# A planned attention and gMLP kernel: the last gelu product of z2 with its sums on VectorE, the centred squares on ScalarE, a longer age for side work

## The chip, the cores and the metric

One core of a Trainium2 chip runs one program. Its engines run side by side, each with an instruction queue of its own that is worked off in order: TensorE (PE: matmuls, and PEld, the load of their weights), VectorE (DVE), ScalarE (ACT), GpSimd (POOL) and SyncE (SP), which here only starts transfers. The metric is the time of one execution on the device in microseconds, the median of several. TensorE alone writes the accumulators in PSUM; POOL reads and writes SBUF only.

## The reference

A block with two branches on the same normalised input is computed, in fp32: attention with 32 heads of 16 columns, and a gMLP whose gate mixes along the sequence. Shapes: x is 2048 x 512, half of the MLP's width is 896.

```python
xn = _layernorm(x)
q, k, v = split(xn @ wqkv)                       # 32 heads, Dh = 16
p = _softmax(q @ k.T * Dh ** -0.5)
attn = merge(p @ v) @ wo
z = _gelu(xn @ w_in)                             # tanh form
z1 = z[..., :Fh]
z2 = _layernorm(z[..., Fh:])
g = w_sp @ z2 + b_sp
return x + attn + (z1 * g) @ w_out
```

The layer norm of z2 is where the change is: mean and variance run over the 896 columns of gelu(z).

## The kernel before

**Precision and slots.** A dense product is made of three fp32r matmuls of high and low parts. Two such matmuls run at a time on the two halves of TensorE's rows: that is a *dense pair* (line 1216), into the accumulator `dps`. A block of scores (`scores`, line 1157) or of row maxima (`maxima`, line 1171) is a pair as well, into one of three PSUM tiles `sl`. ScalarE takes the exponentials of the scores (`pf`), VectorE the maxima (`mm`, line 872); each then frees its `sl`.

**The cycle.** The program is written by a planner in Python. It keeps a clock for each engine and lays out one order for all of them; on the chip only semaphores decide the times. The strings of ORDER say how a *cycle* goes: 8 blocks of scores (S), 7 blocks of maxima in a *short* cycle and 9 in a *long* one (M), 24 dense pairs among them (D), then the P·V block (V, `values`, line 1258): four rounds of matmuls over 8 tiles of exponentials. There are 128 cycles, one behind the other, counted here from 0 by the ends of their P·V blocks. Where no dense pair is ready the planner writes either nothing or a *filler* (line 1230), a pair of matmuls with the zero tile `zeror`. The time of a P·V block, in which neither new scores nor maxima are made, is called a *gap* below, since ScalarE and VectorE have room in it.

**Stages.** The dense work runs through a queue of generators: v and q, k (to cycle 12), z2 (`z2_all`, one tile of 128 rows a cycle, 16 tiles from cycle 13), z1 (`z1_all`), the spatial product in four column blocks of `w_sp` (`spatial`, with tiles `wsp` and `zs` loaded ahead), the output projection of the MLP (`mlp_out`) and of attention (`attn_out`). At the end the last four blocks of heads and the outputs follow (`last_pair`, `last_mm`, `last_add`).

**Side work.** What follows a dense product is a generator as well: `yield "A", t` asks for t microseconds of ScalarE, `"D"` of VectorE, `"G"` of POOL, `"C"` waits for a condition such as a free buffer. `advance` starts, at each planned moment, the task that is ready, by priority. Side work (priority 2) on ScalarE and VectorE (GATED) is gated by `may`: it starts only in a gap, or once it has waited longer than AGE:

```python
return k[3] < 2 or k[0] not in GATED or window[0] <= s0 <= window[1] or s0 - k[2] > AGE
```

**z2.** For a tile `z2_out` copies the two halves out of `dps` (ScalarE and VectorE), and `z2_norm` does the rest: x², its polynomial, the tanh, the product, statistics, r = 1/sqrt, the normalised tile in two column parts as high and low parts (`z2hl`), and their stores to `z2scr`, which SP issues. Each tile holds two of the 19 buffers `big` (`z`, and `u` until the gelu is done); `z2_all` starts a further tile only while more than one is free.

Of the kernel before, what the change touches and what calls it, by code (L numbers as in the profile page):

```python
# [8 lines left out]
F32 = mybir.dt.float32  # L9
F32R = mybir.dt.float32r  # L10
AF = mybir.ActivationFunctionType
ALU = mybir.AluOpType
# [4 lines left out]
P = 128  # L17
S = 2048
D = 512
H = 32  # L20
DH = 16
FH = 896
# [7 lines left out]
EPS = 1e-5  # L30
# [30 lines left out]
def fused_block(ctx, tc, x, wqkv, wo, w_in, w_spT, b_sp, w_out, out):  # L61
    nc = tc.nc
# [3 lines left out]
    sm = ctx.enter_context(tc.tile_pool(name="small", bufs=1))  # L66
# [10 lines left out]
    def act(out, in_, func, **kw):  # L77
        return nc.scalar.activation(out, in_, func, **kw)  # L78

    def ta(n):  # L80
        return 0.2 + n / 1220.0
# [69 lines left out]
    def after(us, fn, *args):  # L151
        at(ends[0] + us, fn, *args)
# [15 lines left out]
    def open_(tag):  # L168
        return "C", lambda: room[tag] > 0

    def lease(tag, n):
        room[tag] += n
# [58 lines left out]
    def hilo(nm):  # L231
        return big.tile([P, 2, 512], F32R, tag="hilo", name=nm, bufs=3)
# [267 lines left out]
    def z2_out(t, z, j):  # L500
        if j == 0:
            yield "A", ta(448)
            act(z[:, 0:448], dps[:, 0, :448], AF.Copy)
        else:
            yield "D", td(448)
            nc.vector.tensor_copy(z[:, 448:896], dps[:, 1, :448])
        rel()
        if not held[0]:
            spawn(z2_norm(t, z), 2, ends[0] + 0.08)

    def z2_norm(t, z):
# [12 lines left out]
        nc.gpsimd.tensor_scalar(u, u, 1.0, 1.0, ALU.add, ALU.mult)  # L524
        yield "G", 2.1
        nc.gpsimd.tensor_mul(z, u, z)
        lease("big", 1)
        st = sm.tile([P, 2, 6], F32, tag="zst", name=f"zst{t}", bufs=6)
        mv = sm.tile([P, 2], F32, tag="zmv", name=f"zmv{t}", bufs=6)
        rs = sm.tile([P, 3], F32, tag="zrs", name=f"zrs{t}", bufs=6)  # L530
        for j in range(2):
            yield "D", 0.62
            nc.vector.bn_stats(st[:, j, :], z[:, j * 448:(j + 1) * 448])
        yield "D", 0.1
        nc.vector.bn_aggr(mv, st)
        yield "G", 1.6
        g = nc.gpsimd
        v, r, q, m = rs[:, 0:1], rs[:, 1:2], rs[:, 2:3], mv[:, 0:1]
        g.tensor_scalar(v, mv[:, 1:2], 1.0, 4 * EPS, ALU.mult, ALU.add)
        g.tensor_tensor(r, v, mhalf, ALU.pow)  # L540
        g.tensor_scalar(q, r, r, v, ALU.mult, ALU.mult)
        g.tensor_scalar(q, q, -0.5, 1.5, ALU.mult, ALU.add)
        g.tensor_mul(r, r, q)
        g.tensor_scalar(q, m, r, -1.0, ALU.mult, ALU.mult)
        for j, (lo, w) in enumerate(((0, 512), (512, 384))):
            yield open_("hilo")
            lease("hilo", -1)
            hl = hilo(f"z2hl{t}_{j}")
            yield "G", 0.0012 * w
            g.tensor_scalar(hl[:, 0, :w], z[:, lo:lo + w], r, q, ALU.mult, ALU.add)  # L550
            yield "G", 0.0012 * w
# [490 lines left out]
    with tc.manual_schedule(engines=engines):  # L1042
# [259 lines left out]
        while n_pv < N or queue or tasks or late or urgent or turn or slots:  # L1302
            t = T["P"]
# [74 lines left out]
```

## Time and profile before

| what | value |
|---|---|
| median of 3 runs | 1856.94 us (1855.68 to 1857.37) |
| the profiled execution | 1855.84 us |
| its span, first to last instruction | 1853.9 us |
| mean granted clock of TensorE | 0.999 |
| ScalarE, exponentials `pf`, 1024 of them | 1026 ns each |
| ScalarE, Square and tanh of a z2 tile | 946 and 953 ns |
| transfers, mean rate | 165 GB/s |

The profile's page gives busy time and count for each engine, the chain of work that ended last, and groups of instructions of one line with their shapes: `out<-in`, count, busy time in all, mean of one in ns, and the idle time of the engine before them with what ended it. A view of stretches gives, for windows that are asked for, length, busy time and count in the order PE, PEld, DVE, ACT, POOL, then TensorE's granted clock, the share of the DMA engines and GB/s. A timeline row has start, duration, engine, line, operation, and in brackets the idle time before it. The clock is full in every stretch that is used here, so it plays no part.

### The profile page before, as it was taken

How to read it: one execution, taken by the hardware profiler on the slowest of the kernel's cores; microseconds unless marked ns; L12 is line 12 of the kernel's file. 1: busy time of each engine (PE TensorE's matmuls, PEld its weight loads, DVE VectorE, ACT ScalarE, POOL GpSimd, SP SyncE). 2: the span in 40 equal slices, each digit the busy share in tenths (PEclk: the TensorE clock that was granted, in tenths of full speed). 3: DMA queues.
4: the chain of work that ended last, by engine and by line, in shares of the span. 5: the costliest groups of instructions: out<-in, count | busy, mean ns of one | idle time of the engine just before them, and what ended most of it. 6: DMA issues, size and time to landing. Idle time of an engine off the chain costs nothing.

```text
span 1853.9 us, 38030 instructions
## 1 busy us (share of the span) xinstructions
PE 1807.5 (97%) x14778; PEld 1093.5 (59%) x14778; DVE 1440.9 (78%) x1677; ACT 1189.6 (64%) x1292; POOL 722.0 (39%) x808
## 2 busy tenths in 40 slices
PE   6999999999999999999999999999999999999998
PEld 4766566655655565556556665666656556565543
DVE  6578778888888787877878787787778878787883
ACT  2157777687776777666666665666656666565665
POOL 5324342778888777222452135102522240002200
PEclk9999999999999999999999999999999999999999
DMA  7728872533565246656867558565767667575422
GB/s 236 288 93 283 277 238 87 127 91 112 133 217 137 100 119 201 152 160 154 219 171 199 156 180 217 155 146 154 194 164 186 177 173 148 149 175 143 130 86 80
DMA packets 212124, 306.14 MB, mean 165 GB/s; under 512 B 36816, under 2 KB 108048, under 8 KB 209056
## 3 DMA queue, kind: packets, MB, share of 16 engines
q1 hardware_dynamic: 202824, 273.83, 53.8%
q0 software_dynamic: 9120, 29.89, 4.7%
q8 instruction: 116, 1.90, 0.4%
q14 instruction: 64, 0.52, 0.1%
HBM read 193.80 MB, written 109.85 MB: 164 GB/s over the span
## 4 chain that ended last, share of the span: by engine, by line
PE 87%; DVE 5%; DMA 2%; ACT 2%; issue 1%; POOL 1%; SPq 1%; DVEq 0%; ACTq 0%; POOLq 0%
PE dps L1216 35%; PE sl L1258 23%; PE sl L1157 14%; PE sl L1171 12%; DVE mm L872 3%; SPq L134 1%; PE dps L1230 1%; ACT pf L78 1%; DMA zs<-z2scr 1%; POOL wsp L293 0%; DMA wsp_11r<-in_w_spT 0%; PE sl L247 0%; PE sl L246 0%; PE sl L245 0%; PE sl L1016 0%
## 5 line engine op out<-in xcount | busy, mean ns | idle before, releaser
L872 DVE TENSOR_REDUCE mm<-sl 128x2 f32<-128x1024 f32 x1024 | 1223.8, 1222 | 202.2 <-PE sl L1171 195.8
L78 ACT ACTIVATE pf<-sl 128x1024 f32<-128x1024 f32 x1024 | 1041.6, 1026 | 335.1 <-PE sl L1157 298.5
L1258 PE MATMUL sl<-pf,vall 128*32 128x512 f32 x4096 | 467.9, 595 | 1.0 <-DVE on L1006 0.6
L1157 PE MATMUL sl<-qst,kst 50*128 50x512 f32 x2048 | 436.0, 418 | 9.4 <-DVE mm L872 2.9
L1171 PE MATMUL sl<-kst,qst 48*128 48x512 f32 x2048 | 422.1, 405 | 4.5 <-DVE mm L872 2.4
L1216 PE MATMUL dps<-wsp,zs 64*128 64x512 f32 x2352 | 379.0, 392 | 1.6 <-DMA zs<-z2scr 1.5
L1157 PEld LDWEIGHTS sl<-qst,kst 50*128 50x128 f32 x2048 | 194.3, 184 | 221.9 <-issue 79.6
L1258 PEld LDWEIGHTS sl<-pf,vall 128*32 128x32 f32 x4096 | 119.3, 109 | 266.9 <-issue 234.3
L1171 PEld LDWEIGHTS sl<-kst,qst 48*128 48x128 f32 x2048 | 195.1, 185 | 105.0 <-ACT pf L78 52.6
L1216 PEld LDWEIGHTS dps<-wsp,zs 64*128 64x128 f32 x2352 | 226.9, 187 | 39.3 <-DMA zs<-z2scr 2.2
L78 ACT ACTIVATE e<-sl 128x512 f32<-128x512 f32 x64 | 38.3, 598 | 205.2 <-PE sl L1258 198.0
L1280 DVE TENSOR_TENSOR e<-sl,e 128x512 f32<-128x512 f32 x64 | 44.3, 692 | 134.3 <-PE sl L1258 76.3
L778 POOL TENSOR_TENSOR hhl<-z1i,hhl 128x512 fp32r<-128x512 f32 x28 | 36.1, 1297 | 267.1 <-ACT hhl L78 267.0
L1216 PE MATMUL dps<-w,xt 64*128 64x448 f32 x768 | 110.4, 368 | 1.5
L1216 PE MATMUL dps<-wout,hp 64*128 64x512 f32 x672 | 110.5, 393 | 0.0
L923 POOL TENSOR_TENSOR ob<-ob 128x512 f32<-128x512 f32 (+1 forms) x16 | 20.6, 1285 | 195.2 <-DMA ob<-rscr 195.2
L1216 PEld LDWEIGHTS dps<-w,xt 64*128 64x128 f32 x768 | 73.5, 186 | 16.3 <-issue 7.8
L1216 PEld LDWEIGHTS dps<-wout,hp 64*128 64x128 f32 x672 | 65.8, 187 | 9.2
L919 POOL TENSOR_TENSOR ob<-ob 128x512 f32<-128x512 f32 (+1 forms) x16 | 20.6, 1287 | 101.6 <-DMA ob<-escr 100.9
L443 POOL TENSOR_TENSOR qkhl<-qr,qkhl 128x512 fp32r<-128x512 f32 x24 | 30.3, 1282 | 70.4 <-ACT qkhl L78 66.3
L1216 PE MATMUL dps<-wf,zs 64*128 64x512 f32 x336 | 55.5, 393 | 0.1
L1216 PE MATMUL dps<-xnT,wqk 64*128 64x512 f32 x288 | 47.7, 396 | 1.1 <-ACT vall L78 0.4
(289 smaller groups left out, 1688.3 us busy)
## 6 DMA issues: line engine op xcount, KB each, us to landing
zs<-z2scr SPq DMA_DIRECT2D x192, 256.0 KB
escr<-e SPq DMA_DIRECT2D x60, 256.0 KB
hscr<-hhl POOLq DMA_DIRECT2D x28, 512.0 KB, 6.4
qst<-qscr SPq DMA_DIRECT2D x30, 384.0 KB
kst<-kscr SPq DMA_DIRECT2D x30, 384.0 KB
qscr<-qkhl SPq DMA_DIRECT2D x16, 512.0 KB
kscr<-qkhl SPq DMA_DIRECT2D x16, 512.0 KB
xscr<-xnT POOLq DMA_DIRECT2D x16, 512.0 KB, 4.8
```

What stands on the lines that cost most here:

```text
L78: return nc.scalar.activation(out, in_, func, **kw)
L134: nc.sync.dma_start(raw(dst), raw(src))
L443: nc.gpsimd.tensor_sub(hl[:, 1, :], raw_, hl[:, 0, :].bitcast(F32))
L778: nc.gpsimd.tensor_sub(hl[:, 1, :], z1, hl[:, 0, :].bitcast(F32))
L872: nc.vector.tensor_reduce(mmax[g][:, :, t, kc], sl[k], AX.X, ALU.max)
L919: nc.gpsimd.tensor_add(both_[rows, 0, :], both_[rows, 0, :], both_[rows, 1, :])
L923: nc.gpsimd.tensor_mul(both_[rows, 0, :], both_[rows, 0, :], both_[rows, 1, :])
L1157: nc.tensor.matmul(sl[k][:, j, :], kst[p % 2][rows, kt * P:(kt + 1) * P], qst[p % 2][rows, c * 512:(c + 1) * 512], start=True, stop=True)
L1171: nc.tensor.matmul(sl[k][:, j, :], qst[p % 2][rows, tt * P:(tt + 1) * P], kst[p % 2][rows, kc * 512:(kc + 1) * 512], start=True, stop=True)
L1216: nc.tensor.matmul(dps[:, bank, :w], lhs, rhs, start=go, stop=stop)
L1258: nc.tensor.matmul(sl[k][cols:cols + VW, 0, :], vpack(kt + r, 2 * p + j), pf[:, j * 512:(j + 1) * 512], start=n % CYC == 0, stop=n % CYC = ...
L1280: nc.vector.tensor_add(e, sl[k][:, 0, :], e)
```

## The change

Three things in the text of the program:

1. In `z2_norm` the last product of the gelu, (tanh + 1)·z, moves from POOL (a pass over 896 columns and a product) to VectorE: one `scalar_tensor_tensor` for each half of 448 columns, which also gives the half's sum. BN_STATS and BN_AGGR go. POOL makes minus the mean of the two sums, ScalarE squares the tile less its mean and sums that, and POOL's short chain for r uses this sum. The buffer `u` is kept until the squares are done.
2. The microseconds that the planner takes for POOL's steps of z2 are changed.
3. AGE goes from 6 to 9, for all side work on ScalarE and VectorE.

```diff
-AGE = 6.0
+AGE = 9.0
...
-        yield "G", 1.0
+        yield "G", 0.98
         nc.gpsimd.tensor_scalar(u, u, 0.044715, 1.0, ALU.mult, ALU.add)
-        yield "G", 2.1
+        yield "G", 2.2
         nc.gpsimd.tensor_mul(u, u, z)
         yield "A", ta(FH)
         act(u, u, AF.Tanh, scale=GC)
-        yield "G", 1.2
-        nc.gpsimd.tensor_scalar(u, u, 1.0, 1.0, ALU.add, ALU.mult)
-        yield "G", 2.1
-        nc.gpsimd.tensor_mul(z, u, z)
+        st = sm.tile([P, 5], F32, tag="zst", name=f"zst{t}", bufs=6)
+        rs = sm.tile([P, 3], F32, tag="zrs", name=f"zrs{t}", bufs=6)
+        g = nc.gpsimd
+        a, b, m, square, v = (st[:, i:i + 1] for i in range(5))
+        for j, half in enumerate((a, b)):
+            cols = slice(j * 448, (j + 1) * 448)
+            yield "D", 0.63
+            nc.vector.scalar_tensor_tensor(z[:, cols], u[:, cols], 1.0, z[:, cols], ALU.add, ALU.mult, accum_out=half)
+        yield "G", 0.6
+        g.tensor_scalar(m, a, b, -1.0 / FH, ALU.add, ALU.mult)
+        yield "A", ta(FH) + 0.2
+        act(u, z, AF.Square, bias=m, accum_out=square)
         lease("big", 1)
...
-        for j in range(2):
-            yield "D", 0.62
-            nc.vector.bn_stats(st[:, j, :], z[:, j * 448:(j + 1) * 448])
-        yield "D", 0.1
-        nc.vector.bn_aggr(mv, st)
-        yield "G", 1.6
...
+        yield "G", 2.2
+        r, q = rs[:, 1:2], rs[:, 2:3]
+        g.tensor_scalar(v, square, 1.0 / FH, 4 * EPS, ALU.mult, ALU.add)
...
-        g.tensor_scalar(q, m, r, -1.0, ALU.mult, ALU.mult)
+        g.tensor_mul(q, m, r)
...
-            yield "G", 0.0012 * w
+            yield "G", 0.0009 * w + 0.32
...
-            yield "G", 0.0025 * w
+            yield "G", 0.0022 * w + 0.24
```

The planner writes another order with it. Three places:

TensorE, the beginning of cycle 22 in the z2 stage, behind the last row of a P·V block (`pf`, `vall`). `qst`/`kst` to `sl` are scores and maxima, `w` and `xt` the weights and the input of a z2 tile. Before:

```order
L1258 MATMUL sl_203<-pf_4471,vall 32x512 x2
L1157 MATMUL sl_202<-qst_90,kst_92 128x512 x2
L1171 MATMUL sl_201<-kst_93,qst_91 128x512 x2
L1230 MATMUL dps<-brow,zeror 128x512 x2
L1157 MATMUL sl_203<-qst_90,kst_92 128x512 x2
L1230 MATMUL dps<-brow,zeror 128x512 x2
L1171 MATMUL sl_202<-kst_93,qst_91 128x512 x2
L1230 MATMUL dps<-brow,zeror 128x512 x2
```

and now:

```order
L1257 MATMUL sl_201<-pf_4492,vall 32x512 x2
L1156 MATMUL sl_203<-qst_90,kst_92 128x512 x2
L1170 MATMUL sl_202<-kst_93,qst_91 128x512 x2
L1215 MATMUL dps<-w_0_0_2669,xt_4184 128x448
L1215 MATMUL dps<-w_0_1_2670,xt_4184 128x448
L1215 MATMUL dps<-w_0_0_2669,xt_4184 128x448
L1215 MATMUL dps<-w_0_1_2670,xt_4184 128x448
L1156 MATMUL sl_201<-qst_90,kst_92 128x512 x2
```

Where cycle 22 had 14 fillers and no dense pair, it has the 24 pairs of a tile and one filler. Counted to the end, the stage has no empty cycle any more and the later stages stand one cycle earlier. At the starts of column blocks 1, 2 and 3 of the spatial product, where before a cycle of 19, 19 and 16 dense pairs stood ahead of two or three cycles with 26 or 27, two cycles of 12 stand ahead of ordinary ones at blocks 1 and 2, and none at block 3; from cycle 89 on the dense work stands one cycle later than before. In all there are 146 matmuls on `zeror` in place of 206.

ScalarE and VectorE, the gap behind a short cycle of the z2 stage. `z2u` are the squares and tanh of a tile, `zst` the sums, `e` the partial output of the P·V block. ScalarE before, from the last exponential of the cycle on:

```order
L78 ACTIVATE pf_4303<-sl_202 128x1024
L78 ACTIVATE z_7_4202<-dps 128x448
L78 ACTIVATE z2u_4320<-z_7_4202 128x896
L78 ACTIVATE z2u_4136<-z2u_4136 128x896
L78 ACTIVATE e_2_4346<-sl_201 128x512
L78 ACTIVATE pf_4362<-sl_203 128x1024
```

and now:

```order
L78 ACTIVATE z_7_4189<-dps 128x448
L78 ACTIVATE pf_4311<-sl_202 128x1024
L78 ACTIVATE z2u_3982,zst_4167<-z_5_3856,zst_4167 128x896
L78 ACTIVATE z2u_4153<-z2u_4153 128x896
L78 ACTIVATE z2u_4315<-z_7_4189 128x896
L78 ACTIVATE e_2_4360<-sl_202 128x512
L78 ACTIVATE pf_4379<-sl_201 128x1024
```

Three side activations stand in the gap where two stood. On VectorE two tiles share such a gap; the second half of one and both halves of the next, now:

```order
L871 TENSOR_REDUCE mm_4635<-sl_202 128x2
L530 SCALAR_TENSOR_TENSOR z_8_4370,zst_4668<-z2u_4486,z_8_4370 128x448
L530 SCALAR_TENSOR_TENSOR z_9_4522,zst_4833<-z2u_4648,z_9_4522 128x448 x2
L1279 TENSOR_TENSOR e_3_4693<-sl_203,e_3_4693 128x512
L871 TENSOR_REDUCE mm_4635<-sl_201 128x2
```

Before, up to four BN_STATS and two BN_AGGR stood there. The first half of the one tile stands in the gap behind the long cycle.

TensorE, the end of the program (`sel`, `on` and `e` belong to the last heads). Before:

```order
L1258 MATMUL sl_201<-pf_20006,vall 32x512 x2
L1258 MATMUL sl_201<-pf_20014,vall 32x512 x2
L1230 MATMUL dps<-brow,zeror 128x512 x2
L1016 MATMUL sl_202<-sel,on_19792 128x512 x2
L1016 MATMUL sl_203<-sel,on_19916 128x512 x2
L1000 MATMUL sl_201<-e_3_19966,sel 32x128 x8
L1230 MATMUL dps<-brow,zeror 128x512 x8
```

and now:

```order
L1257 MATMUL sl_202<-pf_19905,vall 32x512 x2
L1257 MATMUL sl_202<-pf_19913,vall 32x512 x2
L1215 MATMUL dps<-wo_18339,op_1_19695 128x512 x2
L1015 MATMUL sl_203<-sel,on_19674 128x512 x2
L1015 MATMUL sl_201<-sel,on_19811 128x512 x2
L999 MATMUL sl_202<-e_3_19861,sel 32x128 x8
L1215 MATMUL dps<-wo_18339,op_1_19695 128x512 x4
L1215 MATMUL dps<-wo_18340,op_1_19695 128x512 x6
```

The last dense pairs of `attn_out` now stand behind the last P·V block, where fillers stood.

More of the change, by code (lines that the diff above doesn't have):

```diff
@@ L522, in z2_norm @@
         act(u, u, AF.Tanh, scale=GC)
-        yield "G", 1.2
-        nc.gpsimd.tensor_scalar(u, u, 1.0, 1.0, ALU.add, ALU.mult)
-        yield "G", 2.1
-        nc.gpsimd.tensor_mul(z, u, z)
-        lease("big", 1)
-        st = sm.tile([P, 2, 6], F32, tag="zst", name=f"zst{t}", bufs=6)
-        mv = sm.tile([P, 2], F32, tag="zmv", name=f"zmv{t}", bufs=6)
-        rs = sm.tile([P, 3], F32, tag="zrs", name=f"zrs{t}", bufs=6)
-        for j in range(2):
-            yield "D", 0.62
-            nc.vector.bn_stats(st[:, j, :], z[:, j * 448:(j + 1) * 448])
-        yield "D", 0.1
-        nc.vector.bn_aggr(mv, st)
-        yield "G", 1.6
-        g = nc.gpsimd
-        v, r, q, m = rs[:, 0:1], rs[:, 1:2], rs[:, 2:3], mv[:, 0:1]
-        g.tensor_scalar(v, mv[:, 1:2], 1.0, 4 * EPS, ALU.mult, ALU.add)
+        st = sm.tile([P, 5], F32, tag="zst", name=f"zst{t}", bufs=6)
[10 more added lines that the diff above has]
+        act(u, z, AF.Square, bias=m, accum_out=square)
+        lease("big", 1)
+        yield "G", 2.2
+        r, q = rs[:, 1:2], rs[:, 2:3]
+        g.tensor_scalar(v, square, 1.0 / FH, 4 * EPS, ALU.mult, ALU.add)
         g.tensor_tensor(r, v, mhalf, ALU.pow)
@@ L548, in z2_norm @@
             hl = hilo(f"z2hl{t}_{j}")
-            yield "G", 0.0012 * w
+            yield "G", 0.0009 * w + 0.32
             g.tensor_scalar(hl[:, 0, :w], z[:, lo:lo + w], r, q, ALU.mult, ALU.add)
-            yield "G", 0.0012 * w
+            yield "G", 0.0009 * w + 0.32
             g.tensor_scalar(z[:, lo:lo + w], z[:, lo:lo + w], r, q, ALU.mult, ALU.add)
-            yield "G", 0.0025 * w
+            yield "G", 0.0022 * w + 0.24
             nc.gpsimd.tensor_sub(hl[:, 1, :w], z[:, lo:lo + w], hl[:, 0, :w].bitcast(F32))
```

## The prediction

> **What bounds the kernel now.** First the page's busy line, the chain of work that ended last, and VectorE's largest group of instructions (busy us in all, mean ns, idle before it and what ended it).
>
> ```profile
> span 1853.9 us, 38030 instructions
> ...
> PE 1807.5 (97%) x14778; PEld 1093.5 (59%) x14778; DVE 1440.9 (78%) x1677; ACT 1189.6 (64%) x1292; POOL 722.0 (39%) x808
> ...
> PE 87%; DVE 5%; DMA 2%; ACT 2%; issue 1%; POOL 1%; SPq 1%; DVEq 0%; ACTq 0%; POOLq 0%
> ...
> L872 DVE TENSOR_REDUCE mm<-sl 128x2 f32<-128x1024 f32 x1024 | 1223.8, 1222 | 202.2 <-PE sl L1171 195.8
> ```
>
> TensorE is on the chain for 87% of the span. Its 97% needs care, since a matmul that sits in the pipeline counts as busy. So I cut the trace at the ends of the P·V blocks into 128 cycles and read the view of stretches, one cycle to a row (us; busy time and count for each engine). A short cycle has 7 blocks of maxima, a long one 9; both have 8 blocks of scores and 3.57 us of P·V. What varies is the number of dense pairs and of filler pairs. The rows, in order: cycles 22 to 25 (z2 stage), 39 and 40 (z1 stage), 45 to 47, and two ordinary ones of the spatial stage.
>
> ```profile
> 409.82:423.21 13.39, 13.15 (x98) 6.01 (x95) 12.51 (x17) 8.09 (x8) 12.39 (x21) 1.00 0.39 116
> 423.21:436.19 12.98, 12.77 (x115) 8.31 (x111) 9.57 (x10) 10.91 (x12) 12.25 (x18) 1.00 0.35 99
> 436.19:450.65 14.46, 14.10 (x121) 8.71 (x117) 12.91 (x17) 8.42 (x9) 13.22 (x17) 1.00 0.42 124
> 450.65:464.65 14.00, 13.65 (x119) 8.56 (x116) 10.65 (x13) 12.04 (x14) 7.40 (x9) 1.00 0.32 91
> 646.14:659.43 13.29, 13.21 (x115) 8.00 (x111) 9.13 (x8) 10.22 (x12) 9.59 (x11) 1.00 0.47 160
> 659.43:673.25 13.82, 13.73 (x118) 8.08 (x114) 12.61 (x16) 9.71 (x11) 9.46 (x11) 1.00 0.78 173
> 727.64:740.83 13.19, 13.19 (x117) 8.23 (x113) 8.49 (x7) 9.73 (x11) 12.86 (x15) 1.00 0.71 208
> 740.83:754.27 13.44, 13.42 (x102) 6.57 (x98) 11.87 (x15) 8.16 (x8) 6.98 (x8) 1.00 0.66 204
> 754.27:766.78 12.51, 12.51 (x104) 6.48 (x100) 8.31 (x7) 8.53 (x9) 5.16 (x6) 1.00 0.22 58
> 996.35:1009.29 12.94, 12.94 (x114) 8.08 (x110) 8.93 (x9) 8.70 (x9) 1.28 (x1) 1.00 0.68 146
> 1009.29:1022.95 13.66, 13.66 (x120) 8.16 (x116) 11.94 (x15) 8.18 (x8) 3.90 (x4) 1.00 0.68 185
> ```
>
> Two regimes are seen. In the last two rows the cycle is made of TensorE's slots: 8 + 9 + 24 + 1 filler = 42 pairs in 13.66 - 3.57 = 10.09 us, 0.24 us a pair; 39 pairs in 12.94 - 3.57 = 9.37 us give 0.24 again. But a cycle with few dense pairs doesn't get much shorter: with none at all and 14 fillers it is 13.39 (first row), with 12 and 4 fillers 13.44. There the maxima (L872, 1.222 us each, 9 of them 11.0 us) and the three slots `sl` set the pace. An empty cycle is therefore worth about 1 us itself, and costs the 24 pairs (5.8 us) that have to be done in another one.
>
> The first row is the stall that the change is near: no dense pair is issued in cycle 22, and POOL is busy for 12.39 of its 13.39 us.
>
> **The change part by part.** *POOL.* Per z2 tile it loses the pass of L524 and the product of L526, and gets one operation on 128x1.
>
> ```profile
> L524 POOL TENSOR_SCALAR z2u<-z2u 128x896 f32<-128x896 f32 x16 | 15.0, 940 | 31.7 <-ACT z2u L78 31.5
> L526 POOL TENSOR_TENSOR z<-z2u,z 128x896 f32<-128x896 f32 x16 | 33.8, 2110 | 0.3
> ```
>
> That is 0.94 + 2.11 = 3.05 us less in each of 16 tiles, less what the small one takes: some 45 us of the 218 that POOL works in the z2 stretch (below). None of it is on the chain by itself; it ends the empty cycle 22, as the order shows.
>
> *VectorE.* Out: two BN_STATS and a BN_AGGR; in: two SCALAR_TENSOR_TENSOR on 448 columns with both inputs in SBUF.
>
> ```profile
> L533 DVE BATCH_NORM_STATS2 zst<-z 128x6 f32<-128x448 f32 x32 | 18.9, 611 | 3.1 <-POOL z L526 3.1
> ...
> L756 DVE SCALAR_TENSOR_TENSOR z1i<-dps,z1i 128x512 f32<-128x512 f32 x24 | 15.4, 685 | 3.5 <-PE dps L1216 3.5
> ...
> L915 DVE TENSOR_TENSOR os<-os x16: 176/181/1032, 818.0 to 1761.8; 128x32 f32<-128x32 f32 x12, 96x32 f32<-96x32 f32 x4
> ...
> 898.86 1.27 POOL L778 TENSOR_TENSOR hhl<-z1i,hhl 128x512 fp32r<-128x512 f32 x1 [22.03 <-ACT hhl L78]
> 899.15 1.03 DVE L915 TENSOR_TENSOR os<-os 128x32 f32<-128x32 f32 x1
> ```
>
> L756 is the nearest form; at 448 columns 685 x 448/512 = 0.60 us, plus something for the sum: 0.62. The other bound is in L915, the one DVE operation of the long stages with both inputs in SBUF: 0.18 us in the median, but 1.03 where it began under a POOL operation, and it ended with that one (898.86 + 1.27 = 900.13; 899.15 + 1.03 = 900.18). So a hold by POOL can add 0.85, and the upper bound is 1.47 us. I take 0.62 for the operation and holds as below. The Trainium skill ("SBUF — State Buffer", section "SBUF: two separate sides") says that VectorE with two SBUF inputs and GpSimd take one port pair in turn, whole instructions at a time; these rows agree (1.03 against 0.18). By that rule any of the 32 could be held, at most 32 x 0.85 = 27 us of VectorE's time.
>
> What of it reaches TensorE depends on the room in the P·V block, where nearly all of these operations stand. Two such gaps of before, after a short and after a long cycle:
>
> ```profile
> 464.84 0.69 DVE L1280 TENSOR_TENSOR e<-sl,e 128x512 f32<-128x512 f32 x1 [1.21 <-PE sl L1258]
> ...
> 477.94 0.62 DVE L533 BATCH_NORM_STATS2 zst<-z 128x6 f32<-128x448 f32 x1
> 479.89 1.23 DVE L872 TENSOR_REDUCE mm<-sl 128x2 f32<-128x1024 f32 x1 [1.33 <-PE sl L1171]
> ...
> 462.11 0.94 ACT L78 ACTIVATE z2u<-z2u 128x896 f32<-128x896 f32 x1
> ...
> 465.22 1.02 ACT L78 ACTIVATE pf<-sl 128x1024 f32<-128x1024 f32 x1 [1.33 <-PE sl L1157]
> ...
> 461.08:464.65 3.57, 3.57 (x35) 0.94 (x34) 2.51 (x6) 2.70 (x3) 1.31 (x5) 1.00 0.02 5
> 475.54:479.11 3.57, 3.57 (x34) 0.93 (x32) 2.99 (x5) 0.00 (x0) 3.49 (x4) 1.00 0.17 42
> ```
>
> VectorE is free for 1.21 us in the first gap and 1.33 in the second. In the first, three of the new operations (1.86) stand where three BN_STATS (1.83) and two small BN_AGGR stood, and POOL works only 1.31 of 3.57; in the second, where POOL works 3.49 of 3.57, one stands for one BN_STATS, and a hold of 0.85 fits into 1.33. Queued behind them are the sum of the partial outputs (L1280) and the next maxima, for which TensorE waits.
>
> *ScalarE.* One Square with a sum more per tile. Lower bound 0.94 (the same function without a sum). Upper bound, should the sum be read out by an instruction of its own, plus the smallest ACTIVATE of the kernel:
>
> ```profile
> L344 ACT ACTIVATE rs<-mv,epst 128x2 f32<-128x2 f32 x8 | 2.4, 295 | 22.1 <-DVE mv L342 22.1
> ```
>
> so 0.94 to 1.24, against 1.33 us free in the first gap. It fits, barely; behind it stand the exponentials. For both engines I take **+1.0** in all (0 if everything fits; up to 1.4 in each of 8 gaps, 11, if each VectorE operation takes its upper bound: 3 x 1.47 - 1.83 - 1.21 = 1.4).
>
> *The gate (AGE).* In the order 102 of ScalarE's 112 side activations (those that read no PSUM) stood in a P·V gap already, so that the gate has ten to move, in 128 cycles. I cost it at nothing: the gaps hide them, and without that cover an activation among the exponentials is 0.6 to 0.9 us that the next one is late, mostly in ScalarE's own idle time. The stores of z2 (`z2scr`, issued by SP) and all other transfers are the same in number and kind.
>
> *The order that comes of it.* Matmuls are the same in number, but for the fillers: 206 rows of `zeror` before, 146 now, 30 pairs less.
>
> ```profile
> 285.09:577.82 292.73, 285.19 (x2344) 172.50 (x2340) 239.62 (x294) 211.61 (x234) 217.89 (x271) 1.00 0.47 133
> 507.33:577.82 70.49, 67.66 (x544) 38.51 (x540) 56.56 (x69) 49.08 (x55) 62.01 (x84) 1.00 0.67 201
> 914.77:982.65 67.88, 67.75 (x572) 40.80 (x569) 51.97 (x57) 44.16 (x46) 34.48 (x37) 1.00 0.65 178
> 1130.05:1200.06 70.01, 68.36 (x570) 41.02 (x566) 50.94 (x55) 43.43 (x45) 17.24 (x18) 1.00 0.67 166
> 1306.68:1390.35 83.67, 83.15 (x691) 49.62 (x687) 63.02 (x72) 52.01 (x54) 28.47 (x29) 1.00 0.69 176
> 1143.04:1159.74 16.70, 15.11 (x125) 8.91 (x122) 12.44 (x17) 8.14 (x8) 1.26 (x1) 1.00 0.66 148
> 1361.82:1377.41 15.59, 15.20 (x124) 8.99 (x121) 12.93 (x17) 9.09 (x10) 6.76 (x7) 1.00 0.63 161
> 954.79:969.26 14.47, 14.36 (x126) 8.69 (x122) 12.39 (x17) 8.16 (x8) 1.29 (x1) 1.00 0.57 134
> ...
> 1151.66 0.50 PE L1216 MATMUL dps<-wsp,zs 64*128 64x512 f32 x1 [1.17 <-DMA zs<-z2scr]
> ```
>
> I price the new cycles by the rows of their class.
> - Cycles 13 to 33 (z2 and the start of z1) took 292.73. Now: 7 short cycles without filler at 12.98, one with two at 14.00, 8 long ones at 14.46, then three short at 13.3 and two long at 13.85: 90.9 + 14.0 + 115.7 + 67.6 = 288.2, a gain of 4.5. The last five took 70.5 before (the second row), with waits for fetched rows; half of that difference may come back: **-3.0**.
> - Starts of a column block: cycles 59 to 63 took 67.88; now 13.19 + 13.44 + 12.51 + 13.66 + 12.94 = 65.7. 75 to 79 took 70.01; now 12.51 + 13.44 + 12.94 + 13.5 + 13.19 = 65.6. 88 to 93 took 83.67; now 13.5 + 13.19 + 13.66 + 12.94 + 13.5 + 13.19 = 80.0. (13.5: 41 pairs, 13.66 less one.) Together -10.3. Two of their cycles were longer than their class: 76 (16.70) and 92 (15.59) against 14.47 of cycle 62, all long and with 27 dense pairs. The excess, 2.2 + 1.1 = 3.4, is waits for transfers (the last row shows one) that the new order may meet as well; I give half of it back: **-8.6**.
> - The output projection of the MLP (cycles 102 to 117) has a filler in every long cycle before and none now: 7 x 0.24: **-1.7**.
> - The end: dense work is one cycle late from cycle 89 on, so that 18 pairs now stand in the last two cycles where 19 fillers were, 24 pairs against 19, 1.2 us; and one more sum (L967, the row below) stands among the last ones on VectorE. Partly side by side: **+2.0** (1.2 to 2.4).
>
> ```profile
> L967 DVE TENSOR_TENSOR fin<-dps,fin 128x1024 f32<-128x1024 f32 x8 | 9.7, 1216 | 0.7 <-PE dps L1216 0.6 <-issue 0.2
> ```
>
>
> Sum: 1.0 - 3.0 - 8.6 - 1.7 + 2.0 = -10.3. A second, coarser count, which uses no class: 30 pairs at 0.24 = -7.2. I take the middle, -8.8. The profiled execution took 1855.84 (median 1856.94, within 0.1%): 1847.0.
>
> **The rivals.**
> *The gaps of the z2 stage overrun* (slower). The three side operations of ScalarE and those of VectorE no longer fit into the P·V block, by holds and sums, and exponentials and maxima start late. For it: 0.1 to 0.4 us free on ScalarE, 1.03 against 0.18 at L915. Against: POOL's idle first gap. It decides from 12 us in 16 gaps, 0.8 each. At 1.0 each: 1855.84 - 9.8 + 16 = 1862. The Trainium skill ("Vector Engine (DVE) Microarchitecture Reference", section "Points that are easy to get wrong") speaks for it: it has this instruction at half speed with two fp32 sources in SBUF, an estimate of 0.47 us more each. No run here shows such a one; by it alone three would use up just the 1.21 us.
> *The freed slots are waits anyway* (no change). Loads of `wsp` and `zs` need their time whatever TensorE does; then the second term falls to nothing: 1855.84 - 1.7 = 1854. For it: the wait of 1.17 us. Against: in 59 to 63 no such wait is seen.
> *The waits go altogether* (more). No half is given back and the gaps fit: -10.3 - 1.0 - 1.5 - 1.7 = -14.5: 1841.
>
> **How the numbers follow.** Forecast 0.50, slower 0.20, no change 0.14, more 0.16. 0.2% is 3.7 us, about what a measurement tells from none. Faster 0.66, same 0.14, slower 0.20. The forecast's own range is 1843 to 1852; 1839 to 1860 leaves out the worse half of the overrun and a corner below.
>
> **What would show it.** Cycle 22 with 24 dense pairs and POOL some 45 us lower in the z2 stretch; short cycles of it at 13.0, long ones at 14.5 (the overrun: 1 us above both, with ScalarE or VectorE named before `sl`); SCALAR_TENSOR_TENSOR near 0.62 (held: 1 and above); cycles 75 to 79 near 66; an end some 2 us longer. It is wrong if z2's cycles grow by more than 0.6 each, or if the waits for `zs` at the column blocks stay.

## The result, and the profile after

| | median | lowest and highest | runs |
|---|---|---|---|
| before | 1856.6 us | 1854.1, 1858.4 | 9 |
| after | 1846.87 us | 1845.6, 1854.0 | 9 |
| ratio | 0.9957 | 95% interval 0.9945 to 0.9968 | |

By the medians the change gains 9.7 us (0.5%), by the ratio in the table 0.4%. Forecast was 1847.0, a gain of 8.8 (the middle of the sum, 10.3, and the coarse count, 7.2).

The execution that was profiled took 1851.1 us and is one of three of the nine above 1850; a second profile of the same program, taken with the experiments, took 1845.59. The first one's page (busy time, chain of work that ended last):

```profile
span 1849.3 us, 37992 instructions
...
PE 1802.6 (97%) x14718; PEld 1089.7 (59%) x14718; DVE 1440.7 (78%) x1693; ACT 1208.6 (65%) x1324; POOL 681.4 (37%) x792
...
PE 87%; DVE 5%; DMA 3%; issue 1%; ACT 1%; POOL 1%; SPq 0%; DVEq 0%; ACTq 0%; POOLq 0%
```

The chain is what it was; TensorE is 5 us less busy, with 60 matmuls fewer. POOL lost 41 us, ScalarE got 19 more. Source lines after the edited place are one lower than before (the maxima are L871, dense pairs L1215, fillers L1229).

Four cycles of the z2 stage, 22 to 25, in the view of stretches of that execution (us; busy time and count of PE, PEld, DVE, ACT, POOL; clock; share of the DMA engines; GB/s):

```profile
411.49:426.09 14.60, 14.10 (x121) 8.72 (x117) 12.91 (x19) 11.68 (x15) 12.24 (x22) 1.00 0.30 89
426.09:439.06 12.97, 12.76 (x116) 8.23 (x112) 10.53 (x14) 11.18 (x13) 8.28 (x10) 1.00 0.52 148
439.06:453.70 14.64, 14.14 (x120) 8.73 (x117) 12.91 (x20) 11.67 (x15) 12.25 (x22) 1.00 0.30 90
453.70:466.67 12.97, 12.76 (x114) 8.30 (x110) 10.52 (x14) 11.16 (x13) 8.27 (x10) 1.00 0.50 144
```

Cycle 22 has its 24 pairs and costs 14.60 (13.39 when it was empty). Short cycles are 12.97, also cycle 25, which took 14.00; long ones are 14.6 instead of 14.46.

The same view for the stretches of the forecast: cycles 13 to 33, 59 to 63, 75 to 79, 88 to 93, 102 to 117.

```profile
287.41:576.58 289.17, 282.65 (x2356) 175.10 (x2352) 239.31 (x311) 229.80 (x269) 191.74 (x271) 1.00 0.50 140
914.33:980.59 66.26, 65.94 (x538) 37.71 (x534) 52.24 (x58) 43.87 (x46) 27.13 (x29) 1.00 0.51 148
1128.29:1197.99 69.70, 67.71 (x536) 38.72 (x532) 50.34 (x53) 43.82 (x45) 14.82 (x16) 0.98 0.57 144
1305.23:1386.71 81.48, 80.78 (x682) 49.15 (x678) 64.06 (x72) 52.34 (x54) 37.19 (x39) 1.00 0.80 199
1494.09:1707.75 213.66, 213.29 (x1799) 128.54 (x1796) 174.19 (x189) 135.28 (x137) 30.21 (x35) 1.00 0.64 162
```

POOL works 192 us in the first row, 26 less than before and not 45, mostly because work of the z1 stage, which now comes a cycle earlier, has moved into it. The third row is hardly shorter than before (70.01). Its cycle 76 holds one wait, here from the timeline of TensorE (start, duration, engine, line, operation, idle before it and what ended that), and the clock of the cycle fell to 0.90, in its row of the stretches below:

```profile
1150.46 0.49 PE L1170 MATMUL sl<-kst,qst 48*128 48x512 f32 x1 [1.35 <-DMA kst<-kscr]
```

```profile
1141.01:1158.24 17.23, 15.28 (x102) 7.66 (x99) 11.93 (x15) 8.27 (x9) 0.00 (x0) 0.90 0.61 152
```

The second execution has the same order without that wait. Its rows for cycles 13 to 33 and 75 to 79:

```profile
283.77:572.99 289.22, 282.68 (x2356) 175.29 (x2352) 239.41 (x311) 229.87 (x269) 192.19 (x271) 1.00 0.50 140
1126.54:1192.70 66.16, 65.91 (x538) 37.60 (x534) 50.36 (x53) 43.78 (x45) 12.76 (x14) 1.00 0.59 145
```

The new operations, grouped by line and form (busy us in all, mean ns, idle before): two products a tile, ScalarE's square with its sum, and the instructions that read the sums out.

```profile
L530 DVE SCALAR_TENSOR_TENSOR z<-z2u,z 128x448 f32<-128x448 f32 x32 | 19.1, 619 | 4.7 <-ACT z2u L78 4.7
L78 ACT ACTIVATE z2u<-z,zst 128x896 f32<-128x896 f32 x16 | 16.7, 1045 | 0.1
...
L78 ACT ACTIVATION_READ_ACCUMULATOR z2u<-z,zst 128x1 f32 x16 | 3.2, 202 | 0.0
L530 DVE DVE_READ_ACCUMULATOR z<-z2u,z 128x1 f32 x32 | 2.6, 82 | 0.0
```

Where the time came from, by differences to before (us):

| cycles | forecast | first execution | second |
|---|---|---|---|
| 0 to 12 | 0 | +2.3 | -1.3 |
| 13 to 33 (z2, start of z1) | -2.0 | -3.6 | -3.5 |
| 34 to 58, 80 to 87, 94 to 101 | 0 | +2.3 | +2.2 |
| 59 to 63, 75 to 79, 88 to 93 | -8.6 | -4.1 | -8.1 |
| 64 to 74 | 0 | +0.3 | +2.2 |
| 102 to 117 | -1.7 | -2.8 | -2.6 |
| 118 to the last instruction | +2.0 | +1.0 | +1.0 |
| span | -10.3 | -4.6 | -10.1 |

### The profile page after: what moved, and what is told of

Same layout as the page of the kernel before. It is cut to its first block, busy times and chain, and to the rows that moved or that the text cites. A ratio compares the mean times of both kernels' runs of the same rounds, so it can differ in the third digit from the quotient of the medians.

```text
span 1849.3 us, 37992 instructions
## 1 busy us (share of the span) xinstructions
PE 1802.6 (97%) x14718; PEld 1089.7 (59%) x14718; DVE 1440.7 (78%) x1693; ACT 1208.6 (65%) x1324; POOL 681.4 (37%) x792
## 4 chain that ended last, share of the span: by engine, by line
PE 87%; DVE 5%; DMA 3%; issue 1%; ACT 1%; POOL 1%; SPq 0%; DVEq 0%; ACTq 0%; POOLq 0%
PE dps L1215 34%; PE sl L1257 24%; PE sl L1156 14%; PE sl L1170 12%; DVE mm L871 4%; PE dps L1229 1%; ACT pf L78 1%; DMA mscr<-ms 1%; DMA kst<-kscr 1%; DMA qst<-mscr 1%; SPq L134 0%; DMA ob<-rscr 0%; PE sl L247 0%; PE sl L246 0%; DMA wsp_12r<-in_w_spT 0%
## 5 line engine op out<-in xcount | busy, mean ns | idle before, releaser
L871 DVE TENSOR_REDUCE mm<-sl 128x2 f32<-128x1024 f32 x1024 | 1225.3, 1223 | 190.5 <-PE sl L1170 181.6
L1215 PE MATMUL dps<-wsp,zs 64*128 64x512 f32 x2352 | 383.2, 392 | 0.0
L1215 PEld LDWEIGHTS dps<-wsp,zs 64*128 64x128 f32 x2352 | 229.9, 187 | 33.0
L1215 PE MATMUL dps<-w,xt 64*128 64x448 f32 x768 | 110.6, 368 | 1.7
L1215 PE MATMUL dps<-wout,hp 64*128 64x512 f32 x672 | 110.9, 392 | 0.0
L1215 PEld LDWEIGHTS dps<-w,xt 64*128 64x128 f32 x768 | 74.0, 186 | 16.1 <-issue 8.4
L1215 PEld LDWEIGHTS dps<-wout,hp 64*128 64x128 f32 x672 | 64.7, 187 | 9.4
L1215 PE MATMUL dps<-wf,zs 64*128 64x512 f32 x336 | 54.5, 392 | 0.0
L1215 PE MATMUL dps<-xnT,wqk 64*128 64x512 f32 x288 | 47.8, 396 | 1.1 <-ACT vall L78 0.4
```

The lines of the kernel that those rows point to most:

```text
L871: nc.vector.tensor_reduce(mmax[g][:, :, t, kc], sl[k], AX.X, ALU.max)
L1215: nc.tensor.matmul(dps[:, bank, :w], lhs, rhs, start=go, stop=stop)
```

## The experiments

Three questions: which part of the change gains, whether POOL's load counts by itself or only through the order that is made from it, and what the full gaps cost. Each kernel is compared with runs of before on its own chip (medians 1855.6 to 1857.7).

| kernel | median | ratio to before, 95% | cycles 13 to 33 |
|---|---|---|---|
| the change again | 1846.83 | 0.9944 (0.9926 to 0.9961) | 289.2 |
| its operations, old gate | 1865.79 | 1.0041 (1.0027 to 1.0055) | 299.4 |
| gate 9 alone | 1866.21 | 1.0044 (1.0029 to 1.0058) | 296.0 |
| one POOL pass less, old gate | 1865.28 | 1.0037 (1.0025 to 1.0050) | 303.7 |
| one POOL pass less, gate 7 | 1859.87 | 1.0021 (1.0010 to 1.0031) | 302.2 |
| gate 7 alone | 1855.14 | 0.9991 (0.9982 to 1.0001) | 290.3 |
| the change, gate 7 | 1846.86 | 0.9949 (0.9935 to 0.9963) | 289.5 |
| the change, POOL's passes back (u) | 1872.89 | 1.0096 (1.0079 to 1.0113) | 315.3 |
| the change, POOL's passes back (z) | 1861.96 | 1.0040 (1.0025 to 1.0055) | 305.7 |
| the change, old costs | 1847.07 | 0.9955 (0.9943 to 0.9967) | 290.2 |
| the change, square on 128x1 | 1846.12 | 0.9951 (0.9939 to 0.9963) | 288.8 |
| product on VectorE, sums not folded in | 1861.86 | 1.0029 (1.0018 to 1.0041) | 295.9 |

**The change once more.** No edit.

> The changed kernel once more, for a profile without the 1.35 us wait and the lower clock of cycle 76 that the first profile shows. If those belong to that execution alone, the profiled time lies near 1847, cycle 76 near 15.5 and cycles 75 to 79 near 68; if they come of the change, cycle 76 stays near 17.2 and the profiled time near 1851. Ratio to before 0.995 to 0.997 in either case.

The wait belongs to the one execution: cycles 75 to 79 are 66.16, 2 us below the 68 that was expected, and cycle 76 takes 13.5. The second execution is held up elsewhere instead, by 0.81 us behind the P·V block of cycle 65, where a load of `qst` is waited for as well (0.46 us), and in cycle 66 (cycles 64 to 74 take 149.6 us, 147.4 before).

**Operations and gate apart.**

In the change:

```diff
-AGE = 9.0
+AGE = 6.0
```

and in the kernel before:

```diff
-AGE = 6.0
+AGE = 9.0
```

> The changed operations with the old gate (AGE 6). Its order has 121 filler pairs against 73 of the change and 103 of before, two half-filled cycles (20 and 21: 15 and 9 dense pairs) in the z2 stretch, and the same late cycles at the column blocks as before. Theory 1 (the gain comes through the order: cycles filled with dense pairs, fewer fillers): 48 filler pairs x 0.24 = 11.5 us above the change by the coarse count, so about 1858, no gain against before. Theory 2 (the gain is the 45 us that POOL loses and the operations' own times, whatever the order): near 1848, as the change.

> The old operations with the new gate (AGE 9). Its order has 100 filler pairs, cycle 22 stays empty of dense pairs (and two more are split), and some 45 dense pairs stand behind the last P.V block, where before has few. Theory 1 (order): fillers -3 x 0.24 = -0.7, the tail up to 45 x 0.24 = 10.8 longer: 1858 to 1867, slower. Theory 2 (the gate is what gains, by keeping activations out of the blocks of exponentials): faster than before by 5 or more, 1850 or less.

Each half alone is slower than before by 0.4%. The gate alone lies in theory 1's range, the operations alone are slower than either theory has it. With the operations alone, the stretch of cycles 13 to 33 takes 299.44 and a long cycle of it, 24, takes 15.09:

```profile
285.36:584.80 299.44, 289.51 (x2380) 175.87 (x2377) 242.76 (x310) 226.55 (x266) 185.36 (x262) 1.00 0.47 134
...
441.36:456.45 15.09, 14.35 (x124) 8.91 (x120) 12.37 (x16) 9.71 (x13) 13.54 (x24) 1.00 0.29 87
```

In the timeline of ScalarE in that cycle the new square stands among the exponentials:

```profile
447.00 2.12 ACT L78 ACTIVATE pf<-sl 128x1024 f32<-128x1024 f32 x2 [0.40 <-PE sl L1156]
449.01 1.03 ACT L78 ACTIVATE z2u<-z,zst 128x896 f32<-128x896 f32 x1
449.95 0.19 ACT L78 ACTIVATION_READ_ACCUMULATOR z2u<-z,zst 128x1 f32 x1
450.24 0.54 ACT L78 ACTIVATE z<-dps 128x448 f32<-128x448 f32 x1
450.68 1.94 ACT L78 ACTIVATE pf<-sl 128x1024 f32<-128x1024 f32 x2
```

The two exponentials at 450.68 come behind 1.2 us of side work and a copy, and the weights of the P·V block (PEld) wait for them:

```profile
452.88 0.16 PEld L1257 LDWEIGHTS sl<-pf,vall 128*32 128x32 f32 x8 [0.36 <-ACT pf L78]
```

The cycle also has three fillers where the change has one. Of the 48 squares and tanh of z2, some 19 start outside a gap here and 10 in the change, eight of these only 0.5 to 1.1 us ahead of a P·V block. The total (1865.8) is 8 us above the coarse count's 1858: the counted fillers don't hold these delays.

With the gate alone the rows are those of cycles 13 to 33, 75 to 79, and of the end, from the first round of the last P·V block to TensorE's last matmul (16.75 before):

```profile
285.58:581.60 296.02, 285.63 (x2354) 173.58 (x2350) 239.60 (x294) 211.83 (x234) 216.73 (x266) 1.00 0.47 132
...
1135.01:1201.72 66.71, 66.45 (x538) 37.73 (x535) 50.63 (x55) 43.14 (x44) 33.36 (x36) 1.00 0.55 152
...
1831.21:1858.79 27.58, 25.96 (x194) 13.62 (x190) 12.27 (x12) 5.16 (x6) 0.00 (x0) 1.00 0.39 135
```

So the shorter column blocks come with a gate of 9 and the old operations too, where they start one cycle later than before; in the change they start one earlier. Being early is therefore not what makes them short. Part of it is work that is put off: cycles 59 to 63 hold 121 dense pairs before and 97 in both of these. With the gate alone the late dense work is paid at the end, 10.8 us for 45 pairs (0.24 each), and the z2 stretch is 3.3 longer than before.

**One POOL pass less.** The pass of 0.94 us is taken out of before, with the old gate and with a gate of 7.

```diff
-        yield "G", 1.2
-        nc.gpsimd.tensor_scalar(u, u, 1.0, 1.0, ALU.add, ALU.mult)
```

> The kernel before with POOL's pass of L524 (the 1 that is added to the tanh) left out, so that z2 lacks that term; nothing else changed, old gate. Its order has 89 filler pairs against 103, cycle 22 has its 24 dense pairs, and dense work is done early at the end. Theory 1 (POOL's load made the empty cycle, and the order carries the gain): 14 x 0.24 = 3.4 less by the coarse count, and the stretch of cycles 13 to 33 some 3 to 4 us shorter: 1851 to 1854. Theory 2 (the new forms of VectorE and ScalarE are what gains): no change, 1856.

> The kernel before without POOL's pass of L524 (the 1 that is added to the tanh is left out of z2), this time with the gate at 7 instead of 6. Its order has 76 filler pairs, no empty cycle, the same late cycles as the change (45/46, 60/61, 75/76), 18 dense pairs in the last two cycles. Theory A (the change gains by POOL's relief and the gate together, through the order; the new forms on VectorE and ScalarE are not needed for it): z2 stretch within 2 us of the change's 289.2, the whole within 3 us of 1846.8: 1845 to 1850. Theory B (the new forms carry the gain): no faster than before, 1856 or more.

With fewer fillers than before (89, 76) and no empty cycle both kernels are slower. With the old gate both theories miss; with the gate of 7 theory B's number comes true (1856 or more), though the rows show another reason than B's. The z2 stretch is what grows (second kernel):

```profile
284.16:586.35 302.19, 287.29 (x2361) 174.96 (x2358) 241.10 (x295) 212.87 (x237) 217.69 (x271) 0.99 0.47 134
```

and a tanh in a gap shows why, in the timelines of POOL, ScalarE and TensorE (L1155 are the scores here):

```profile
424.34 2.10 POOL L520 TENSOR_TENSOR z2u<-z2u,z 128x896 f32<-128x896 f32 x1
...
426.47 0.95 ACT L78 ACTIVATE z2u<-z2u 128x896 f32<-128x896 f32 x1 [4.36 <-POOL z2u L520]
427.33 0.93 ACT L78 ACTIVATE z2u<-z 128x896 f32<-128x896 f32 x1
428.17 0.58 ACT L78 ACTIVATE e<-sl 128x512 f32<-128x512 f32 x1
...
428.80 0.50 PE L1155 MATMUL sl<-qst,kst 50*128 50x512 f32 x2 [1.14 <-ACT e L78]
```

The P·V block ends at 426.1; the tanh starts only then because POOL is late, the next partial output and exponentials stand behind two side activations, and TensorE waits. It looks as if the order was made for a POOL that is faster than POOL is: the six small operations are planned at 1.6 us and take about 2.2. (In before the pass that is missing here was planned at 1.2 us and took 0.94, which may have made up for it.) No run with the true costs tries this. Outside the z2 stretch this kernel gains like the change: 66.3, 68.1 and 81.3 at the column blocks.

**The gate at 7.**

> The kernel before with the gate at 7: 101 filler pairs, cycle 22 empty, late cycles and end as before. Theory A: the gate without POOL's relief gives nothing: 1855 to 1859 (2 filler pairs less, 0.5). Theory B (the gate keeps activations away from the exponentials and gains by that alone, and the gate at 9 only lost by its 45 dense pairs at the end): 1850 or less.

> The change with the gate at 7 instead of 9: 71 filler pairs against 73, the same cycles otherwise. Theory A (what counts is on which side of a step of the order the gate lies, somewhere between 6 and 6.5 for the new operations; beyond it nothing more comes): as the change, 1845 to 1848. Theory B (the longer gate itself gains, the more the longer): between the old gate's 1866 and the change's 1847, 1850 or more.

As theory A has it. The old operations keep the empty cycle 22 at this gate and gain nothing that can be told from none; the new ones need the gate above 6, and 9 brings no more than 7. One thing theory A doesn't say: in the profiled execution of the old operations at 7 (1852.98 us) cycles 13 to 33 take 290.3, only 1 us more than in the change. What doesn't come there are the shorter column blocks: they take 67.9, 69.8 and 84.1, start in the same cycles as before and hold as many dense pairs.

**POOL's load put back, the order kept.** In two places, each with three passes a tile:

```diff
 g.tensor_scalar(m, a, b, -1.0 / FH, ALU.add, ALU.mult)
+for k in range(3):
+    g.tensor_scalar(u, u, 1.0, 0.0, ALU.mult, ALU.add)
...
 g.tensor_mul(q, m, r)
+for k in range(3):
+    g.tensor_scalar(z, z, 1.0, 0.0, ALU.mult, ALU.add)
```

> The change with 3 passes of POOL over z2u (times 1, plus 0; 0.94 us each, 45 us in all) put back behind the small operation that makes the mean, without the order knowing of them: TensorE, VectorE and ScalarE keep the change's order to the row. Theory A (POOL's load costs only through the order that is made from it; its own time is hidden, POOL works 192 of the 289 us of the stretch): z2 stretch at most 3 us longer, 1847 to 1850. Theory C (POOL's time is on the path in the stretch itself, so that the order as planned can't be kept with that load): z2 stretch longer by 8 us or more, 1855 and up, with tanh or stores waiting for POOL.

> The change with the same 3 passes of POOL a tile (45 us in all), now on z behind the six small operations, where neither VectorE nor ScalarE waits for them within the tile (in the run before, ScalarE's square had to wait for them, since it writes z2u, and the run tells little of POOL's load). Order unchanged to the row on the other engines. Theory A (POOL's time itself is hidden): z2 stretch at most 3 us longer, 1847 to 1850. Theory C (POOL has no room left for the 45 us in the order that the change gets, so that tanh in the gap waits for POOL): z2 stretch longer by 8 us or more, 1855 and up, with tanh's idle time ended by L520.

Theory C, twice. The first kernel says little of the load, as its second expectation tells. In the second, cycles 13 to 33:

```profile
284.97:590.66 305.69, 288.85 (x2354) 176.91 (x2350) 242.36 (x311) 229.87 (x269) 244.91 (x319) 0.98 0.48 132
```

and ScalarE in the gap ahead of a long cycle:

```profile
441.39 0.95 ACT L78 ACTIVATE z2u<-z 128x896 f32<-128x896 f32 x1
444.64 1.04 ACT L78 ACTIVATE z2u<-z,zst 128x896 f32<-128x896 f32 x1 [2.31 <-POOL zst L532]
```

It is not tanh that waits, as I had expected, but the new square, for the mean that POOL makes (L532, 0.26 us). That operation stands in POOL's queue behind the normalising of another tile, which the added passes have made late; the exponentials stand behind the square, and TensorE behind the exponentials:

```profile
446.74 0.50 PE L1172 MATMUL sl<-kst,qst 48*128 48x512 f32 x2 [1.85 <-ACT pf L78]
```

53 us more of POOL's time make the stretch 16.5 us longer, though POOL is idle for a fifth of it; all of that lies in seven long cycles. Two things besides the passes are in these numbers: some 8 of the 53 us are POOL's other operations, longer where VectorE's products fall among them, and an estimated 4.4 of the 16.5 us (TensorE's busy time times the clock that is missing) are a lower clock in three of the cycles (last section).

**The planner's costs.**

```diff
-yield "G", 2.2
+yield "G", 1.6
```

for the six small operations, and so with the other costs of POOL that the change touches.

> The change with the planner's old costs for POOL (1.6 instead of 2.2 for the six small operations, 0.0012 w and 0.0025 w for the three passes of a half); operations and gate as in the change. 73 filler pairs and the same late cycles, but 359 rows of difference in ScalarE's order of the z2 stretch. Theory A (the operations and the gate make the gain): 1845 to 1849. Theory D (the true costs are needed: with the old ones POOL is later than planned and tanh, in the gap, waits for it, as in the kernel without the pass and the gate at 7): z2 stretch 3 us longer or more, 1850 to 1860.

Theory A: the new costs are not needed for the gain. Presumably, with the pass and the product off POOL, the error of the old ones finds slack.

**What the third activation in the gap costs.**

```diff
-act(u, z, AF.Square, bias=m, accum_out=square)
+act(square, a, AF.Square, bias=m)
```

> The change with ScalarE's centred square and its sum on 128x1 instead of 128x896 (so that z2's variance is wrong); every engine keeps the change's order to the row. It takes 0.7 us or so out of one gap per tile. Theory A (the third activation overfills only the gap of the long cycle, by 0.15 us a cycle): long cycles of the z2 stretch 14.47 instead of 14.62, 1.2 us in all, 1844.5 to 1846.5. Theory E (the gaps overrun in a way the cycle times hide, the sum's read-out above all): the stretch 5 us shorter or more, 1842 or less.

The kernel leaves out the variance. A miss for A, in its detail, and theory E fails too (the stretch takes 288.8, the change's 289.2). The long cycles stay at 14.6:

```profile
436.46:451.05 14.59, 14.09 (x121) 8.73 (x118) 13.39 (x20) 10.28 (x12) 12.97 (x23) 1.00 0.30 88
```

The gap ahead of it, in the timelines of TensorE and ScalarE:

```profile
435.92 0.61 PE L1257 MATMUL sl<-pf,vall 128*32 128x512 f32 x4
...
435.99 0.29 ACT L78 ACTIVATE zst<-zst 128x1 f32<-128x1 f32 x1
437.03 1.94 ACT L78 ACTIVATE pf<-sl 128x1024 f32<-128x1024 f32 x2 [0.74 <-PE sl L1156]
```

and the same gap in the change (second execution):

```profile
431.87 3.64 PE L1257 MATMUL sl<-pf,vall 128*32 128x512 f32 x32
...
434.97 1.05 ACT L78 ACTIVATE z2u<-z,zst 128x896 f32<-128x896 f32 x1
435.90 0.20 ACT L78 ACTIVATION_READ_ACCUMULATOR z2u<-z,zst 128x1 f32 x1
436.01 1.95 ACT L78 ACTIVATE pf<-sl 128x1024 f32<-128x1024 f32 x2
```

The first exponential starts 0.50 us after the end of the P·V block in both (437.03 - 436.53, 436.01 - 435.51), since its scores aren't there earlier. Without the square ScalarE waits 0.74 us for them; with it the work just fits. So the 0.15 us of a long cycle doesn't come from the square. TensorE's order differs in these cycles (four dense pairs stand ahead of the second block of maxima where before has three), which may be the cause; that was not tried by itself.

**The product without its sums.** VectorE multiplies, BN_STATS and BN_AGGR stay, no centred square; gate and costs as in the change.

```diff
-nc.gpsimd.tensor_scalar(u, u, 1.0, 1.0, ALU.add, ALU.mult)
-nc.gpsimd.tensor_mul(z, u, z)
+for j in range(2):
+    cols = slice(j * 448, (j + 1) * 448)
+    yield "D", 0.55
+    nc.vector.scalar_tensor_tensor(z[:, cols], u[:, cols], 1.0, z[:, cols], ALU.add, ALU.mult)
```

> The product by VectorE as in the change, but its sums not folded in: BN_STATS and BN_AGGR stay, ScalarE makes no centred square. Gate 9, the change's costs. POOL loses the same 45 us. VectorE has four operations of 0.6 a tile in the gaps where the change has two. Its order has 115 filler pairs, two empty cycles (19 and 26) and 45 dense pairs behind the last P.V block. Theory A (POOL's relief with the gate is all that counts): 1850 or less. Theory F (the sums had to be folded into the product, since the gaps have VectorE's room for two operations a tile and not for four): two empty cycles for none, 42 filler pairs x 0.24 = 10 above the change, and up to 10 for the end: 1857 to 1867, slower than before.

The total is in theory F's range, 0.3% slower than before. Cycles 13 to 33, and the end, from the first round of the last P·V block on:

```profile
287.03:582.88 295.85, 286.72 (x2345) 172.98 (x2342) 258.17 (x325) 208.91 (x231) 169.46 (x227) 1.00 0.44 125
...
1831.94:1859.90 27.96, 26.00 (x194) 13.68 (x190) 12.29 (x12) 5.15 (x6) 0.00 (x0) 1.00 0.39 132
```

POOL is relieved here more than in the change (169 us), and two cycles are empty. What the sums in the product save should be VectorE's room in the gaps, as theory F has it. But the run doesn't settle that: the end is 11.2 us longer than before (27.96 against 16.75), more than the whole loss, and such an end comes with a gate of 9 and the old operations too. At a gate of 7, where they have no such end, this kernel was not tried.

## Why the prediction was right, and where it was not

The total and its sign came from reading the new order: which cycles hold how many dense pairs and fillers, priced by the rows of before. That held. That the sum (-10.3) and the second execution (-10.1) agree to 0.2 us is partly luck, since several terms are off by 1 to 2 us and cancel. The terms, one by one:

- **z2 stretch, -3.0 and +1.0 for the gaps.** -3.5 measured. The empty cycle went as said, short cycles are 12.97 (12.98 forecast), and no stall was passed on to the five cycles behind: they take 67.7 instead of 70.5 and make 2.8 of the 3.5. The +1.0 came out right for another reason: the square fits (no excess with or without it), and six of the eight long cycles are some 0.15 longer. POOL is 26 us lower in the stretch, not 45, since z1's work moved in.
- **Durations.** 0.62 for the product: 0.619, and 0.08 more for the read-out of the sum. The square with its sum is 1.05 + 0.20 = 1.25 us, at the upper bound of 1.24.
- **Column blocks, -8.6.** -8.1 in the undisturbed execution, -4.1 in the first. Half of the waits was to come back: in the two executions that were profiled they come at different cycles (76 in the first, 65 and 66 in the second). The rival of freed slots that are waits anyway named the loads of `wsp` and `zs`. Those are not what is seen: the wait for `zs` of 1.17 us is gone in both executions (0.4 us of such waits is left in the second), and the waits there are for `kst` in the first and in part for `qst` in the second, both loaded for the scores and maxima. At 75 to 79 the first execution has nearly the rival's size, by another wait and a lower clock; in the second the slots went.
- **MLP, -1.7.** -2.6 and -2.8: the fillers went, and the cycles behind are a little shorter still.
- **End, +2.0.** +1.0, below its range of 1.2 to 2.4: from the end of the last P·V block to the last instruction it takes 1.4 more, and cycles 118 to 127 give 0.4 of it back.
- **Not in the sum:** +2.2 in three quiet stretches, some 0.2 us in each second or third cycle, where dense pairs and gaps stand in another order. What makes the 0.2 was not tried.

Two steps don't hold in general, though the sum didn't show it.

The first: "I cost it at nothing", of **the gate**. I counted ten activations that it moves in the order of before. With the new operations it decides over many more: at 6 some nineteen z2 activations stand outside the gaps, the stretch grows by 10 us, and the whole is 19 us slower than with 7 or 9 (1865.8 against 1846.8). By the count of fillers 11.5 of these come through the order, which the prediction did price for the gate of 9. The remark that an activation among the exponentials falls "mostly in ScalarE's own idle time" doesn't hold in the 15.09 us cycle, where the P·V block waits 0.36 us for exponentials behind one.

The second: "None of it is on the chain by itself", of **POOL's load**. In the order of before nothing here contradicts it. In the order of the change it fails: with the load back and the order kept, the kernel is 15 us slower than the change. POOL now makes the mean between VectorE's sums and ScalarE's square, and so stands in a chain that has to close within a gap; its queue must be short when that small operation comes.

The rival of the **overrunning gaps** doesn't hold in the change; its mechanism is real. No product of the change was held (614 to 627 ns in the second execution): when one starts, POOL stands idle or works on 128x1 tiles. Where POOL works on whole tiles, as in the experiments, products take up to 2.56 us (one in the change with the gate at 7).

So no part that was tried alone gains clear of the noise, and the gain isn't a sum of parts. The new operations need the gate above 6 (1865.8 against 1846.9 at 7), and the gate at 7 with the old operations, whose order keeps the empty cycle, gives 1855.1. Of the kernels tried none beats the change clear of the noise; the gate at 7 is as fast. Two things stay open: whether the sums have to be in the product, since VectorE's product without them was tried at a gate of 9 alone, and whether one POOL pass less would do with the true costs.

## What to carry to other kernels

Where a planner writes one order from cost estimates, a change of operations, of costs and of thresholds is one change: price the order that comes out, and test its parts with the order held and with the order free. In an engine queue that is worked off in order, a small operation between two engines' work inherits the delay of everything ahead of it, so an engine that is idle for a fifth of the time can still set the pace. Counts of fillers are a good price only while nothing in the order is late.

## What the runs showed of the hardware

**Reading a sum out is an instruction of its own:** 82 ns on VectorE, 202 ns on ScalarE.

**VectorE's product of two fp32 sources in SBUF runs at the rate of the form with one in PSUM:** 619 ns for 448 columns, against 685 for 512 (1.38 and 1.34 ns a column). The estimate of half speed (the Trainium skill, "Vector Engine (DVE) Microarchitecture Reference", section "Points that are easy to get wrong") is not borne out by any run here.

**POOL can hold it for a whole instruction.** In the last experiment, the products of two tiles (min, median and max of 4 in ns), and two rows of the timelines, VectorE's (two products in 2.89 us) and POOL's:

```profile
L526 DVE SCALAR_TENSOR_TENSOR z<-z2u,z x4: 604/620/2351, 381.3 to 400.0; 128x448 f32<-128x448 f32 x4
```

```profile
381.35 2.89 DVE L526 SCALAR_TENSOR_TENSOR z<-z2u,z 128x448 f32<-128x448 f32 x2
...
381.11 2.10 POOL L520 TENSOR_TENSOR z2u<-z2u,z 128x896 f32<-128x896 f32 x1
```

The first product took 2.35 us, to 383.70; POOL's operation ended at 383.21. The remaining 0.49 is a little less than a product's own time, 0.61 in this kernel. With POOL's passes back on u the median over 32 products was 0.98 us, and POOL was slowed as well, 3.48 us for three passes under two products against 2.99 for three without:

```profile
L530 DVE SCALAR_TENSOR_TENSOR z<-z2u,z x32: 615/982/1345, 325.0 to 540.2; 128x448 f32<-128x448 f32 x32
```

```profile
417.79 3.48 POOL L534 TENSOR_SCALAR z2u<-z2u 128x896 f32<-128x896 f32 x3
...
422.70 2.99 POOL L534 TENSOR_SCALAR z2u<-z2u 128x896 f32<-128x896 f32 x3
```

This agrees with the Trainium skill ("SBUF — State Buffer", section "SBUF: two separate sides"): one port pair, taken in turn for whole instructions.

**A cycle with a stall can lose clock on top.** Two long cycles with POOL's passes on z, and a part of the second:

```profile
412.99:429.72 16.73, 14.40 (x122) 8.72 (x118) 13.17 (x20) 12.05 (x15) 15.22 (x23) 1.00 0.39 112
442.68:460.95 18.27, 15.92 (x120) 9.78 (x116) 13.11 (x20) 12.05 (x15) 16.48 (x26) 0.91 0.40 118
...
447.40:450.81 3.41, 3.41 (x20) 2.57 (x16) 2.40 (x2) 1.34 (x3) 3.08 (x6) 0.51 0.57 183
```

TensorE is idle for 2.3 us in each; in the second the granted clock is 0.91 in the mean, and the cycle is 1.5 us longer. The mean hides a short fall: for 3.41 us, from 0.7 us behind the wait of 1.85, the clock is at half (0.51). Of the five long cycles of this kernel with 2.3 us of idle time or more, three have such a fall. Cycle 76 above, with 0.90, is alike. What decides when it falls was not tried.
